# Chunk-selected attention and a softplus MLP: from two phases to one interleaved stream, with head pairs, 256-query steps, casting loads and one activation table

## The chip, the cores and the metric

The kernel runs on one core of one Trainium2 chip. The metric is device time in microseconds (us) of that core, given as the median of the runs of a kernel. Engines are named as in the profile: PE is TensorE, PEld its weight loads, DVE is VectorE, ACT is ScalarE, POOL is GpSimd, SP is SyncE. Lines such as L282 are lines of the kernel's source file; in experiments that add lines the numbers shift by a few.

## The reference, cut to what matters

There are 4 batches of 8 heads, 768 positions and 64 columns per head. Each query may attend to 6 chunks of 32 keys, picked by an upper bound on its scores; the result goes through a 512 to 2048 to 512 MLP with a softplus.

```python
ub = sum(maximum(q * k_min, q * k_max), axis=-1)      # per query and chunk of 32 keys
ub = where(causal_chunk, ub, -1e9)
top_chunks = argsort(ub)[..., -6:]
scores = scale * q @ k.T
scores = where(selected & causal, scores, -1e9)
attn = softmax(scores)
x = (attn @ v) laid out as 3072 tokens x 512
h = x @ w_in                                          # 512 x 2048
g = maximum(h, 0) + log1p(exp(-abs(h)))               # softplus
out = g @ w_out                                       # 2048 x 512
```

## The kernel before: the parts that matter

Attention runs head by head, and after it the MLP runs in blocks of 512 tokens. Both weights are loaded first, as float32, in front of the first q, k and v.

```python
# weights first, float32, then cast on DVE  (... cut)
nc.sync.dma_start(out=w_in_f32, in_=...); nc.vector.tensor_copy(w_in_sb, w_in_f32)
nc.sync.dma_start(out=w_out_f32, in_=...); nc.vector.tensor_copy(w_out_sb, w_out_f32)

# attention, for each of 32 heads, after its setup (... cut), 6 tiles of 128 queries
for tj in range(g0, g1):
    nc.tensor.matmul(at_ps[...], Kaug[0:KK, ...], Qaug[0:KK, ...], start=True, stop=True)
nc.vector.tensor_add(at_ps[diagonal], at_ps[diagonal], ltri)
nc.scalar.activation(attnT[...], at_ps[...], ACT.Exp)
for tj in range(g0, g1):
    nc.tensor.matmul(o_ps, attnT[...], v_aug[:, tj, :], start=(tj == 0), stop=(tj == t))
nc.vector.reciprocal(rrec, o_ps[:, D:D + 1])
nc.scalar.activation(o_sb, o_ps[:, 0:D], ACT.Copy, bias=0.0, scale=rrec)
nc.tensor.transpose(oT_ps, o_sb, ident)

# MLP, after all attention: 6 blocks of 512 tokens
for fg in range(KFF // 2):
    # 8 matmuls of 512 columns into hp (... cut)
    nc.scalar.activation(e_sb, hp, ACT.Exp)
    nc.scalar.activation(gT[...], e_sb, ACT.Ln, bias=1.0)
# then 4 x 16 matmuls with w_out, a copy and a store (... cut)
```

Exp and ln alternate on ACT in the MLP, and the compiled program loads an activation table before nearly each of them.

Of the kernel before, what the change touches and what calls it, by code (L numbers as in the profile page):

```python
# [17 lines left out]
def kernel(  # L18
# [14 lines left out]
    NQT = S // 128  # L33
    scale = 1.0 / math.sqrt(D)
    NEG = -30000.0
# [3 lines left out]
    assert d_model == H * D  # L39
    KDM = d_model // 128  # L40
    KFF = d_ff // 128

    ROWS = D + 1 + NCH

    singles = ctx.enter_context(tc.tile_pool(name="singles", bufs=1))
    ident = singles.tile([128, 128], BF16)
    make_identity(nc, ident)

    ltri = singles.tile([128, 128], F32, name="ltri")
    nc.gpsimd.memset(ltri, 0.0)  # L50
    nc.gpsimd.affine_select(out=ltri, in_=ltri, compare_op=ALU.is_ge, fill=NEG,
                            base=0, channel_multiplier=-1, pattern=[[1, 128]])

    ohb = singles.tile([32, S], BF16, name="ohb")
    nc.gpsimd.memset(ohb, 1.0)
# [3 lines left out]
                            base=CH - 1, channel_multiplier=CH, pattern=[[-1, S]])  # L59

    NKA = 3
    Kaugs = []
    for i in range(NKA):
        ka = singles.tile([128, S], BF16, name=f"Kaug{i}")
        nc.gpsimd.memset(ka[D:D + 64, :], 1.0)
        nc.sync.dma_start(out=ka[D + 1:D + 1 + NCH, :], in_=ohb[0:NCH, :])
        Kaugs.append(ka)

    xT = []
    for p in range(KDM):  # L70
        t = singles.tile([128, NTOK], BF16, name=f"xT_{p}")
        xT.append(t)

    w_in_f32 = singles.tile([128, KDM, d_ff], F32, name="w_in_f32")
    nc.sync.dma_start(out=w_in_f32,
                      in_=moe_w_in.rearrange("(kt ki) f -> ki kt f", ki=128))
    w_in_sb = singles.tile([128, KDM, d_ff], BF16, name="w_in_sb")
    nc.vector.tensor_copy(w_in_sb, w_in_f32)

    w_out_f32 = singles.tile([128, KFF, d_model], F32, name="w_out_f32")  # L80
    nc.sync.dma_start(out=w_out_f32,
                      in_=moe_w_out.rearrange("(kt ki) f -> ki kt f", ki=128))
    w_out_sb = singles.tile([128, KFF, d_model], BF16, name="w_out_sb")
    nc.vector.tensor_copy(w_out_sb, w_out_f32)

    attn_ctx = ExitStack()
    bh_pool = attn_ctx.enter_context(tc.tile_pool(name="bh", bufs=3))
    tp_psum = attn_ctx.enter_context(tc.tile_pool(name="tp_psum", bufs=2, space=bass.MemoryType.PSUM))
    at_psum = attn_ctx.enter_context(tc.tile_pool(name="at_psum", bufs=2, space=bass.MemoryType.PSUM))
    sm_psum = attn_ctx.enter_context(tc.tile_pool(name="sm_psum", bufs=2, space=bass.MemoryType.PSUM))  # L90
    work = attn_ctx.enter_context(tc.tile_pool(name="work", bufs=6))
    work2 = attn_ctx.enter_context(tc.tile_pool(name="work2", bufs=8))

    def do_setup(b, h, bh_idx):
        Kaug = Kaugs[bh_idx % NKA]
        q_f = bh_pool.tile([128, NQT, D], F32, name="q_f")
        nc.sync.dma_start(out=q_f, in_=q[b, h].rearrange("(t s) d -> s t d", s=128))
        k_f = bh_pool.tile([128, NQT, D], F32, name="k_f")
        nc.sync.dma_start(out=k_f, in_=k[b, h].rearrange("(t s) d -> s t d", s=128))
        v_f = bh_pool.tile([128, NQT, D], F32, name="v_f")  # L100
        nc.sync.dma_start(out=v_f, in_=v[b, h].rearrange("(t s) d -> s t d", s=128))

        k_b = bh_pool.tile([128, NQT, D], BF16, name="k_b")
        nc.vector.tensor_copy(k_b, k_f)
        v_aug = bh_pool.tile([128, NQT, D + 1], BF16, name="v_aug")
        nc.scalar.copy(v_aug[:, :, 0:D], v_f)
        nc.gpsimd.memset(v_aug[:, :, D:D + 1], 1.0)

        Qraw = bh_pool.tile([128, NQT, ROWS], BF16, name="Qraw")
        nc.scalar.copy(Qraw[:, :, 0:D], q_f)  # L110

        qT_ps = tp_psum.tile([D, S], BF16, name="qT_ps", tag="tp")
        kT_ps = tp_psum.tile([D, S], BF16, name="kT_ps", tag="tp")
        q_b_ap = Qraw[:, :, 0:D]
        for t in range(NQT):
            nc.tensor.transpose(qT_ps[:, t * 128:(t + 1) * 128],  # L116
                                q_b_ap[:, t, :], ident)
            nc.tensor.transpose(kT_ps[:, t * 128:(t + 1) * 128],  # L118
                                k_b[:, t, :], ident)
        qT = bh_pool.tile([D, S], BF16, name="qT")  # L120
        nc.vector.tensor_copy(qT, qT_ps)
        nc.scalar.activation(Kaug[0:D, :], kT_ps, ACT.Copy, bias=0.0, scale=scale)

        kmaxT = bh_pool.tile([D, NCH], BF16, name="kmaxT")
        kminT = bh_pool.tile([D, NCH], BF16, name="kminT")
        kT3 = Kaug[0:D, :].rearrange("d (c g) -> d c g", g=CH)
        nc.vector.tensor_reduce(kmaxT, kT3, axis=AX.X, op=ALU.max)  # L127
        nc.vector.tensor_reduce(kminT, kT3, axis=AX.X, op=ALU.min)  # L128

        qposT = bh_pool.tile([D, S], BF16, name="qposT")  # L130
        qnegT = bh_pool.tile([D, S], BF16, name="qnegT")
        nc.vector.tensor_scalar_max(qposT, qT, 0.0)
        nc.vector.tensor_scalar_min(qnegT, qT, 0.0)

        ub_ps = sm_psum.tile([128, NQT, NCH], F32, name="ub_ps", tag="sm")
        for t in range(NQT):
            qs = slice(t * 128, (t + 1) * 128)
            nc.tensor.matmul(ub_ps[:, t, :], qposT[:, qs], kmaxT,
                             start=True, stop=False)
            nc.tensor.matmul(ub_ps[:, t, :], qnegT[:, qs], kminT,  # L140
                             start=False, stop=True)
        ub_sb = bh_pool.tile([128, NQT, NCH], F32, name="ub_sb")
        nc.vector.tensor_copy(ub_sb, ub_ps)
        nc.gpsimd.affine_select(
            out=ub_sb, in_=ub_sb, compare_op=ALU.is_ge, fill=NEG,
            base=0, channel_multiplier=1, pattern=[[128, NQT], [-CH, NCH]])

        m8 = bh_pool.tile([128, NQT, 8], F32, name="m8")
        for t in range(NQT):
            nc.vector.max(out=m8[:, t, :], in_=ub_sb[:, t, :])  # L150
        nc.vector.tensor_scalar_mul(Qraw[:, :, D:D + 1], m8[:, :, 0:1], -1.0)
        ltm = bh_pool.tile([128, NQT, NCH], F32, name="ltm")
        nc.vector.tensor_tensor(
            ltm, ub_sb, m8[:, :, TOPK - 1:TOPK].to_broadcast([128, NQT, NCH]),
            op=ALU.is_lt)
        nc.vector.tensor_scalar_mul(Qraw[:, :, D + 1:D + 1 + NCH], ltm, NEG)

        Qaug_ps = tp_psum.tile([ROWS, S], BF16, name="Qaug_ps", tag="tp")
        for t in range(NQT):
            nc.tensor.transpose(Qaug_ps[:, t * 128:(t + 1) * 128],  # L160
                                Qraw[:, t, :], ident)
        Qaug = bh_pool.tile([128, S], BF16, name="Qaug")
        nc.scalar.copy(Qaug[:ROWS, :], Qaug_ps)

        return dict(Kaug=Kaug, Qaug=Qaug, v_aug=v_aug, h=h, b=b)

    def do_qtiles(st):
        Kaug, Qaug, v_aug, h, b = st["Kaug"], st["Qaug"], st["v_aug"], st["h"], st["b"]
        for t in range(NQT):
            nchk = (t + 1) * 4  # L170
            kcols = (t + 1) * 128
            KK = D + 1 + nchk

            attnT = work.tile([128, NQT * 128], BF16, name="attnT", tag="attnT")
            o_ps = sm_psum.tile([128, D + 1], F32, name="o_ps", tag="sm")
            for g0 in range(0, t + 1, 4):
                g1 = min(g0 + 4, t + 1)
                at_ps = at_psum.tile([128, 512], F32, name="at_ps", tag="at")
                for tj in range(g0, g1):
                    nc.tensor.matmul(  # L180
                        at_ps[:, (tj - g0) * 128:(tj - g0 + 1) * 128],
                        Kaug[0:KK, tj * 128:(tj + 1) * 128],
                        Qaug[0:KK, t * 128:(t + 1) * 128], start=True, stop=True)
                if g0 <= t < g1:
                    nc.vector.tensor_add(  # L185
                        at_ps[:, (t - g0) * 128:(t - g0 + 1) * 128],
                        at_ps[:, (t - g0) * 128:(t - g0 + 1) * 128], ltri)
# [19 lines left out]
    for i, (b, h) in enumerate(bhs):  # L207
        cur = do_setup(b, h, i)
        if prev is not None:
            do_qtiles(prev)  # L210
        prev = cur
    do_qtiles(prev)

    attn_ctx.close()

# [63 lines left out]
```

## Time and profile before

| | before |
|---|---|
| median of 3 runs | 688.14 us (687.73 to 689.16) |
| attention, by the timeline | about 27 to 392 us |
| MLP | about 392 to 687 us |
| ACT busy | 432.2 us, of which 106.5 us are table loads |
| PE busy | 494.0 us |

The first lines of the page give the busy time of each engine, and the busy share in 40 equal slices of the span (tenths, 9 is 90% or more). PEclk is the clock granted to PE, in tenths.

```profile
span 687.0 us, 9091 instructions
PE 494.0 (72%) x3248; PEld 276.2 (40%) x3264; DVE 275.9 (40%) x1114; ACT 432.2 (63%) x756; POOL 20.3 (3%) x78
...
PE   0178887778777887888787874965956956757647
...
ACT  0256666567566666666665599199297495693890
...
PEclk9999999755555555555555577897987988988978
```

No engine is full in the first half: from 40 to 380 us PE is busy for 82% and ACT for 62%. In the second half PE and ACT take turns. The chain of work that ended last says the same: it passes among three engines.

```profile
PE 43%; ACT 30%; DVE 18%; issue 6%; POOL 1%; ACTq 0%; DVEq 0%; POOLq 0%
```

The costliest groups give line, engine, operation, output and input, count, then busy us and mean ns, then the idle time of the engine before them and its releaser.

```profile
L197 ACT ACTIVATE o_sb<-o_ps,rrec 128x64 bf16<-128x64 f32 x192 | 59.6, 312 | 80.1 <-DVE rrec L195 79.9
L237 ACT ACTIVATE e_sb<-hp 128x1024 f32<-128x1024 f32 x48 | 48.5, 1022 | 72.1 <-PE hp L231 71.6
...
L231 PE MATMUL hp<-xT_81,w_in_sb 128*128 128x512 bf16 x96 | 40.7, 424 | 47.8 <-ACT e_sb L237 47.2
...
L238 ACT ACT_TABLE_LOAD x42 | 53.9, 1283 | 0.8
L237 ACT ACT_TABLE_LOAD x41 | 52.6, 1283 | 0.7
```

There are 83 table loads of 1.283 us within the MLP. ACT hardly idles before them (0.8 and 0.7 us in all), so they are work, not waiting. The timeline of one step of the MLP's first half-block shows what this does (start, duration, engine, line, operation; in brackets the idle time before it and who ended it).

```profile
404.42 1.28 ACT L237 ACT_TABLE_LOAD   x1
405.71 1.02 ACT L237 ACTIVATE e_sb<-hp 128x1024 f32<-128x1024 f32 x1
406.75 1.28 ACT L238 ACT_TABLE_LOAD   x1
406.79 0.38 PE L231 MATMUL hp<-xT_81,w_in_sb 128*128 128x512 bf16 x1 [2.82 <-ACT e_sb L237]
...
408.05 1.06 ACT L238 ACTIVATE gT<-e_sb 128x1024 bf16<-128x1024 f32 x1
...
408.48 0.63 PE L231 MATMUL hp<-xT_83,w_in_sb 128*128 128x512 bf16 x1
408.91 0.63 PE L231 MATMUL hp<-xT_84,w_in_sb 128*128 128x512 bf16 x1
```

ACT takes 4.6 us for two blocks of 128 hidden columns, more than half of it table loads. PE waits 2.8 us for it. Then the first matmuls follow at 0.215 us for 512 columns, and from 408 us on at 0.43. The Trainium skill ("TensorE: Matmul & The Clock Gate", section "Wait — 56ns, not 53.3ns?") gives start-to-start times of 426.7 ns for 512 columns while the array is cold and 215.7 ns once it is warm, and 106.7 and 55.6 ns for 128. This agrees: 0.43 us here, and the attention's score matmuls ran at about 0.107 us per 128 columns, cold (four of them took 0.62 us at 62.3 us, a single one about 0.30, so (0.62 - 0.30) / 3). The PEclk row still shows 0.9 at 62.3 us. The same page (section "Seeing it yourself") warns that its clock events have been seen to be unreliable.

### The profile page before, as it was taken

The page shows a single profiled execution, that of the slowest core. Times are in us where ns is not written, and L with a number is a line of the kernel's source. Part 1 is how long each engine was busy: PE and PEld are TensorE (multiplying, and loading weights), DVE is VectorE, ACT ScalarE, POOL GpSimd, SP SyncE. Part 2 cuts the span into 40 slices and gives each one's busy share as a digit, 9 for nine tenths or more (in the row PEclk, how much of TensorE's full clock was granted, in tenths as well). Part 3 has the DMA queues.
Part 4 walks back from the last instruction along what each step waited for, and adds up shares of the span by engine and source line. Part 5 has one row for each costly group of instructions (what it writes and reads, how often), then busy time and mean ns, then how long its engine had stood idle before and what let it go on. Part 6 is the DMA issues. An engine that isn't in the chain of part 4 may idle for free.

```text
span 687.0 us, 9091 instructions
## 1 busy us (share of the span) xinstructions
PE 494.0 (72%) x3248; PEld 276.2 (40%) x3264; DVE 275.9 (40%) x1114; ACT 432.2 (63%) x756; POOL 20.3 (3%) x78
## 2 busy tenths in 40 slices
PE   0178887778777887888787874965956956757647
PEld 0155555555555555555555421421422422313213
DVE  1576767676767676676767400100100100001001
ACT  0256666567566666666665599199297495693890
POOL 3000000000000000000000000000000000000000
PEclk9999999755555555555555577897987988988978
DMA  9963222222223221321000000100100100001001
GB/s 336 290 109 72 59 49 56 49 62 54 47 48 70 47 54 40 70 55 39 13 1 1 0 1 0 61 1 0 62 0 15 47 0 31 31 0 46 16 0 61
DMA packets 81465, 34.25 MB, mean 50 GB/s; under 512 B 75716, under 2 KB 75788, under 8 KB 80908
## 3 DMA queue, kind: packets, MB, share of 16 engines
q1 hardware_dynamic: 81420, 33.67, 18.9%
q8 instruction: 25, 0.41, 0.3%
q14 instruction: 20, 0.16, 0.1%
HBM read 27.26 MB, written 6.29 MB: 49 GB/s over the span
## 4 chain that ended last, share of the span: by engine, by line
PE 43%; ACT 30%; DVE 18%; issue 6%; POOL 1%; ACTq 0%; DVEq 0%; POOLq 0%
PE op L242 12%; ACT L238 8%; PE at_ps L180 7%; ACT e_sb L237 7%; ACT L237 7%; ACT gT L238 6%; PE o_ps L191 6%; PE oT_ps L199 5%; PE qT_ps L116 4%; DVE kminT L128 4%; PE Qaug_ps L160 4%; DVE kmaxT L127 4%; DVE at_ps L185 2%; PE kT_ps L118 2%; PE hp L231 2%
## 5 line engine op out<-in xcount | busy, mean ns | idle before, releaser
L242 PE MATMUL op<-w_out_sb,gT 128*128 128x512 bf16 x376 | 100.5, 425 | 40.7 <-ACT gT L238 40.3
L246 DVE COPY mo_sb<-op 128x512 f32<-128x512 f32 x24 | 16.6, 692 | 275.1 <-PE op L242 268.3
L188 ACT ACTIVATE attnT<-at_ps 128x512 bf16<-128x512 f32 (+3 forms) x256 | 109.2, 447 | 24.4 <-PE at_ps L180 17.1
L197 ACT ACTIVATE o_sb<-o_ps,rrec 128x64 bf16<-128x64 f32 x192 | 59.6, 312 | 80.1 <-DVE rrec L195 79.9
L237 ACT ACTIVATE e_sb<-hp 128x1024 f32<-128x1024 f32 x48 | 48.5, 1022 | 72.1 <-PE hp L231 71.6
L191 PE MATMUL o_ps<-v_aug,attnT 128*128 128x65 bf16 x672 | 85.4, 241 | 5.2 <-ACT attnT L188 4.5
L199 PE MATMUL oT_ps<-ident,o_sb 128*64 128x128 bf16 x192 | 59.8, 313 | 40.1 <-ACT o_sb L197 39.6
L231 PEld LDWEIGHTS <-w_in_sb 128*128 128x128 bf16 x384 | 41.1, 107 | 108.0 <-issue 73.6
L242 PEld LDWEIGHTS <-gT 128*128 128x128 bf16 x384 | 39.5, 107 | 102.4 <-ACT gT L238 50.9
L231 PE MATMUL hp<-xT_81,w_in_sb 128*128 128x512 bf16 x96 | 40.7, 424 | 47.8 <-ACT e_sb L237 47.2
L191 PEld LDWEIGHTS <-attnT 128*128 128x128 bf16 x672 | 47.0, 118 | 44.9 <-ACT attnT L188 17.5
L116 PE MATMUL qT_ps<-ident,Qraw 128*64 128x128 bf16 x192 | 38.8, 313 | 26.6 <-ACT Qraw L110 26.6
L185 DVE TENSOR_TENSOR at_ps<-at_ps,ltri 128x128 f32<-128x128 f32 x192 | 53.7, 288 | 6.8 <-PE at_ps L180 1.7
L238 ACT ACT_TABLE_LOAD x42 | 53.9, 1283 | 0.8
L237 ACT ACT_TABLE_LOAD x41 | 52.6, 1283 | 0.7
L199 PEld LDWEIGHTS <-o_sb 128*64 128x64 bf16 x192 | 25.7, 134 | 67.9 <-ACT o_sb L197 58.2
L238 ACT ACTIVATE gT<-e_sb 128x1024 bf16<-128x1024 f32 x48 | 50.0, 1054 | 0.5
L231 PE MATMUL hp<-xT_83,w_in_sb 128*128 128x512 bf16 x96 | 41.8, 436 | 0.7 <-issue 0.7
L195 DVE RECIPROCAL rrec<-o_ps 128x1 f32<-128x1 f32 x192 | 30.9, 161 | 24.7 <-PE o_ps L191 21.3
L180 PE MATMUL at_ps<-Qaug,Kaug_75 89*128 89x128 bf16 (+5 forms) x231 | 40.5, 305 | 0.2 <-ACT attnT L188 0.2
L180 PE MATMUL at_ps<-Qaug,Kaug_72 89*128 89x128 bf16 (+5 forms) x231 | 39.1, 304 | 0.6 <-ACT attnT L188 0.6
L231 PE MATMUL hp<-xT_84,w_in_sb 128*128 128x512 bf16 x92 | 39.6, 430 | 0.0
(151 smaller groups left out, 649.2 us busy)
## 6 DMA issues: line engine op xcount, KB each, us to landing
q_f<-in_q_dram SPq DMA_DIRECT2D x32, 192.0 KB, 2.8
k_f<-in_k_dram SPq DMA_DIRECT2D x32, 192.0 KB, 2.7
v_f<-in_v_dram SPq DMA_DIRECT2D x32, 192.0 KB, 2.8
out_dram<-mo_sb SPq DMA_DIRECT2D x24, 256.0 KB, 2.0
w_in_f_85<-in_moe_w_in_dram SPq DMA_DIRECT2D x1, 4096.0 KB, 12.9
w_out_f_89<-in_moe_w_out_dram SPq DMA_DIRECT2D x1, 4096.0 KB, 16.9
Kaug_72<-ohb SPq DMA_DIRECT2D x1, 36.0 KB
Kaug_75<-ohb SPq DMA_DIRECT2D x1, 36.0 KB
```

Source lines behind the costliest of these rows:

```text
L116: nc.tensor.transpose(qT_ps[:, t * 128:(t + 1) * 128], q_b_ap[:, t, :], ident)
L180: nc.tensor.matmul(at_ps[:, (tj - g0) * 128:(tj - g0 + 1) * 128], Kaug[0:KK, tj * 128:(tj + 1) * 128], Qaug[0:KK, t * 128:(t + 1) * 128], ...
L185: nc.vector.tensor_add(at_ps[:, (t - g0) * 128:(t - g0 + 1) * 128], at_ps[:, (t - g0) * 128:(t - g0 + 1) * 128], ltri)
L188: nc.scalar.activation(attnT[:, g0 * 128:g1 * 128], at_ps[:, :(g1 - g0) * 128], ACT.Exp)
L191: nc.tensor.matmul(o_ps, attnT[:, tj * 128:(tj + 1) * 128], v_aug[:, tj, :], start=(tj == 0), stop=(tj == t))
L195: nc.vector.reciprocal(rrec, o_ps[:, D:D + 1])
L197: nc.scalar.activation(o_sb, o_ps[:, 0:D], ACT.Copy, bias=0.0, scale=rrec)
L199: nc.tensor.transpose(oT_ps, o_sb, ident)
L231: nc.tensor.matmul(hp[:, fi, :], w_in_sb[:, dt, ft * 128:(ft + 1) * 128], xT[dt][:, cs], start=(dt == 0), stop=(dt == KDM - 1))
L237: nc.scalar.activation(e_sb, hp, ACT.Exp)
L238: nc.scalar.activation(gT[:, fg * 2:fg * 2 + 2, :], e_sb, ACT.Ln, bias=1.0)
L242: nc.tensor.matmul(op, gT[:, ft, stt * 128:(stt + 1) * 128], w_out_sb[:, ft, :], start=(ft == 0), stop=(ft == KFF - 1))
```

## The change

Its intent is to make one stream in which MLP matmuls fill the gaps of attention, and to take work off ACT and DVE:

- One activation table that holds exp, ln and copy is loaded once.
- q, k and v of two heads form a pair. They are loaded by casting DMAs on POOL's queue, straight to bf16; the weights too, w_in after the third pair and w_out in the second pair's preparation.
- The chunk bounds of both heads are one matmul against block-diagonal chunk maxima and minima. The chunk mask is a part of the score matmul: one-hot rows stand in the key tile, and masks in the query tile.
- Scores come in steps of 256 queries; the causal diagonal is zeroed by POOL after the exp; the normalising division moved to DVE.
- MLP blocks are 256 tokens, and the program emits MLP pieces between attention pieces by a cost ratio.

```diff
+    nc.scalar.preload_act_table_set("natural_log_exp_and_others")
+    def load(i):                          # load_v(i) likewise
+        for h in range(2):
+            nc.gpsimd.dma_start(out=k_sb[:, :, h, :], in_=k[b, 2 * p + h].rearrange(...))
+            nc.gpsimd.dma_start(out=q_sb[:, :, h, :], in_=q[b, 2 * p + h].rearrange(...))
...
+    for i in range(NV):                   # NV = 12 tiles of V with a column of ones
+        nc.vector.memset(v_sb[i][:, :, :, D:D + 1], 1.0)
+    for i in range(NK):                   # NK = 8 key tiles per head of a pair
+        nc.vector.tensor_copy(KA[i][64:96, :], ohb)
+        nc.vector.memset(KB[i][0:32, :], 0.0)
+        nc.vector.tensor_copy(KB[i][32:64, :], ohb)
+    load(1); load_v(1); load(2); load_v(2)      # after load(0), load_v(0)
+    for kt in range(KDM):
+        nc.gpsimd.dma_start(out=w_in_sb[:, kt, :], in_=moe_w_in[...])
...
+    def prep_pair(i):
+        # 6 transposes of k, max and min per chunk on DVE, key copies on ACT
+        for m, dst in enumerate((kmx, kmn)):
+            for h in range(2):
+                nc.gpsimd.tensor_copy(dst[h * 64:(h + 1) * 64, h], kx[h * 64:(h + 1) * 64, m])
+        yield 0.35
+        # 6 transposes of q; load(i + 3), load_v(i + 3); w_out if i == 1; qpos, qneg on DVE
+        # 12 matmuls: bounds ub; top-6 threshold and masks on DVE; 6 transposes of the masks
...
+    def score_step(st):
+        # two matmuls of up to 256 columns, one exp of 384 or 512 columns, repeated
+        nc.scalar.activation(pt[...], s_ps[:, 0:n], ACT.Exp, scale=scale)
+        nc.gpsimd.affine_select(out=diag, in_=diag, compare_op=ALU.is_ge, fill=0.0, ...)
...
+    RATIO = 1.75
+    def pump(cost):
+        state["attn"] += cost
+        while state["mlp"] < state["attn"] * RATIO - LAG:
+            c = next(mlp, "end")
...
```

An MLP block needs the outputs of all four pairs of its batch, so the MLP can't begin before the fourth pair is prepared.

## The prediction

> **What bounds the kernel now.** Two phases in series. In the windows view attention runs from 26.6 us (PE's first instruction, its loads queued behind 8 MB of weights) to about 383 us, the MLP from there to 687. From 40 to 380 us PE is busy 82%, DVE 70%, ACT 62%, at the cold pitch (128 columns per 0.107 us in the timeline). The chain of waits alternates PE, DVE, ACT inside each 128-query tile. In the MLP's first half-block ACT is the limit: table load 1.28, exp 1.02, load 1.28, ln 1.06 us per 1024 columns; 83 reloads are 106.5 us of ACT's 432. ACT also waits 72 us for the first matmuls of each block (waits view).
>
> **What the change does, costed from the trace.**
> - One table: removes 106.5 us of ACT, nearly all on the path.
> - ACT: the forms fit 0.165 us + 0.00084 per column. 96 exps of 384 (0.488) and 96 of 512 (0.596) are 104 us, 32 key copies (0.8) 26, 96 MLP exps of 512 57, 48 ln 51: 238 us, from 432. The 192 output scalings (59.6), casts (33) and Qaug copies (25) leave ACT.
> - PE: MLP is 384 matmuls at the warm 512-column pitch 0.215 plus 768 at half that (estimate): 166 us. Attention, at warm pitch, my estimate: 85 us, with half the transposes. 250 us, if warm.
> - DVE: about 6.8 us per pair of preparation, 0.9 per step, 0.7 per output: about 175 us, from 276.
> - GpSimd: 96 masks and 64 small copies, about 50 us, plus issuing 104 casting loads, which no trace here shows. The Trainium skill ("DMA: Bandwidth & Descriptors", SWDGE vs HWDGE vs iDMA) says a casting DMA must come from GpSimd, whose cores compute the descriptors. 1 to 2 us each is my guess, so 150 to 250 us of GpSimd.
> - Overlap: MLP matmuls fill attention's gaps; the sum of two latency-bound phases becomes the longest engine plus ramp.
>
> **The sum.** Loads, the preparations of four pairs (DVE 27 us, serial through PE, DVE and GpSimd) and 4 MB of w_in ahead of the fourth pair let the MLP start at about 55 to 65 us, with some 20 us of PE work done. The remaining 230 us run at about 85% of PE, since ACT (218 us left) is nearly as loaded and PSUM has only two score and two h buffers and one each for o and y: 270 us. Tail (last h chunks and outputs, PE-bound, partly in that): about 15. Predicted 345 us, range 300 to 405. Faster by over 2%: 0.97; within 2%: 0.01; slower: 0.02.
>
> **What shows each step.** One table load; ACT busy 230 to 250, PE 250 to 300 by the page, DVE 160 to 190. The 512-column pitch 0.215 in mid-run and a granted clock above 0.9 after 70 us. The chain mostly PE and ACT. First MLP matmul at 50 to 70 us.
>
> **What would make it wrong.** (1) Descriptor generation: at 3 us or more per load GpSimd has 350 us or more and becomes the limit, masks queued behind loads; it would lead the chain of waits. (2) A cold PE: the skill ("TensorE: Matmul & The Clock Gate", Part 1) puts the half-rate clock down to idle windows; this trace agrees, as first MLP matmuls go from 0.215 to 0.43 pitch after a 2.8 us gap. If the interleaved stream pauses often, PE needs up to 500 us. (3) In-order PE waiting on single buffers: 380 or more. (4) A better-packed stream: 300.

## More of the kernel before

The timeline has the last transpose of attention at 391.7 us and the first MLP matmul at 392.3 us.

## The result, and the profile after

| | before | after |
|---|---|---|
| median of the same rounds | 687.93 us (4 runs) | 351.00 us (350.19 to 352.25, 4 runs) |
| ratio | | 0.5104, 95% interval 0.509 to 0.5117 |
| PE busy | 494.0 | 281.8 |
| DVE busy | 275.9 | 171.5 |
| ACT busy | 432.2 | 218.1 |
| POOL busy | 20.3 | 140.1 |

A ratio is the mean time of one kernel's fast runs over that of the other's fast runs of the same rounds, so it isn't quite the ratio of the medians.

The same lines of the page, after. Rows for POOL and for DMA (the busy share of the DMA engines) are added, since both have become part of the story.

```profile
span 350.5 us, 7076 instructions
PE 281.8 (80%) x2784; PEld 202.2 (58%) x2784; DVE 171.5 (49%) x580; ACT 218.1 (62%) x369; POOL 140.1 (40%) x274
...
PE   1003254389889989999999899999999999999994
...
ACT  1102022259879749677987596879876878876640
POOL 8994877961682744350514443101112211000000
PEclk9999999999999999999999999999999999999999
DMA  9999999990795864443703444000000000000111
```

From the ninth slice on PE is busy for 80% or more. Before that, for some 70 us, PE is under 60% and POOL is the busiest of the engines in the sum. The DMA engines are at 90% or more for the first 79 us. The windows view puts numbers to it (window, its length, then busy us and instruction count of PE, PEld, DVE, ACT and POOL, the granted clock, the DMA share and GB/s).

```profile
0.00:80.00 80.00, 28.43 (x231) 20.63 (x232) 46.03 (x156) 17.77 (x29) 63.62 (x105) 1.00 1.40 122
...
100.00:320.00 220.00, 209.66 (x2171) 152.04 (x2171) 107.96 (x367) 171.28 (x296) 67.55 (x152) 1.00 0.32 40
```

PE is busy for 209.66 of 220 us in mid-run, and for 28.43 of the first 80. The chain of work that ended last names all engines.

```profile
PE 49%; POOL 16%; ACT 15%; DMA 7%; issue 7%; DVE 4%; POOLq 0%; ACTq 0%; DVEq 0%
```

In order of time (start, us, what), all of the chain's DMA lies in the first 77 us. It is two pieces, each from the issue of a weight to its landing:

```profile
21.89 11.92 DMA w_in_sb<-in_moe_w_in_dram
41.75 13.20 DMA w_out_sb<-in_moe_w_out_dram
```

They are 25 of these 77 us, and POOL's work is 33; the other 25 us of POOL's share are spread over the stream. After the first piece POOL issues its next load, having paused for 2.0 us. So the transfers of the weights, or full DMA engines, are a rival to POOL's order as the cause of the late start. No run takes the weights out; what the other runs say of it stands after the table of starts.

PE's waits of the first 80 us (engine, what it was for, releaser: us in all, times, longest) name the work on POOL.

```profile
PE ub L182 <- POOL bd_0_151 L151: 14.2, 1, 14.2
PE ub L182 <- POOL bd_1_153 L151: 7.6, 1, 7.6
PE o_ps L244 <- POOL pt L229: 7.3, 5, 3.4
```

The first is the block-diagonal copy of the first pair, a copy of 0.2 us. POOL's timeline shows why it came at 22.4 us: it stood behind the issue of the loads of the second and third pair and of w_in. (Not POOL alone held PE up: the other operand, qpos, was ready only at 21.52 us, since on DVE it stood behind the copies of the one-hot rows.)

```profile
18.27 1.88 POOL L86 DMA_DIRECT2D v_100<-in_v_dram  x2
20.14 2.29 POOL L127 DMA_DIRECT2D w_in_sb<-in_moe_w_in_dram  x4
22.41 0.47 POOL L151 COPY bd_0_151<-kx 64x24 bf16<-64x24 bf16 x2
```

The MLP's first matmul came at 55.42 us, but it was one alone. The unbroken stream begins at 77.07 us, and there the pitch changes from cold to warm.

```profile
78.35 0.42 PE L282 MATMUL hp<-xT_222,w_in_sb 128*128 128x256 bf16 x1
78.56 0.42 PE L282 MATMUL hp<-xT_223,w_in_sb 128*128 128x256 bf16 x1
...
79.62 0.27 PE L282 MATMUL hp<-xT_223,w_in_sb 128*128 128x256 bf16 x1
79.73 0.27 PE L282 MATMUL hp<-xT_224,w_in_sb 128*128 128x256 bf16 x1
```

256 columns take 0.21 us from start to start at 78.4 us, and 0.11 us at 79.6 us. The granted clock reads 1.00 for the whole start, so here too the pitch tells what the column doesn't.

The groups that answer those of before:

```profile
L225 ACT ACTIVATE pt<-s_ps 128x512 bf16<-128x512 f32 (+1 forms) x192 | 99.6, 544 | 69.3 <-PE s_ps L223 68.2
L297 PE MATMUL y<-w_out_sb,g 128*128 128x512 bf16 x384 | 100.4, 379 | 1.6 <-DVE y_sb L302 1.6
...
L284 ACT ACTIVATE e_sb<-hp 128x512 f32<-128x512 f32 x96 | 57.0, 597 | 37.3 <-PE hp L282 36.5
...
L286 ACT ACTIVATE g<-e_sb 128x1024 bf16<-128x1024 f32 x48 | 50.8, 1059 | 0.5
...
L77 POOL DMA_DIRECT2D k_sb<-in_k_dram x32 | 27.3, 855 | 25.5 <-PE kT L142 21.3
```

The waits have become one-sided. Before, ACT's exps of the MLP waited for PE (71.6 us) and PE waited for ACT's exps (47.2 us). Now the exps still wait for PE (36.5 us), while PE idles for 0.4 us in all before the matmuls of that layer. Issuing one load costs POOL 0.855 us.

### The profile page after: what moved, and what is told of

It is laid out like the page before. It is cut to its first block, busy times and chain, and to the rows that moved or that the text cites. A ratio compares the mean times of both kernels' runs of the same rounds, so it can differ in the third digit from the quotient of the medians.

```text
span 350.5 us, 7076 instructions
## 1 busy us (share of the span) xinstructions
PE 281.8 (80%) x2784; PEld 202.2 (58%) x2784; DVE 171.5 (49%) x580; ACT 218.1 (62%) x369; POOL 140.1 (40%) x274
## 3 DMA queue, kind: packets, MB, share of 16 engines
q0 software_dynamic: 77952, 13.64, 49.7%
## 4 chain that ended last, share of the span: by engine, by line
PE 49%; POOL 16%; ACT 15%; DMA 7%; issue 7%; DVE 4%; POOLq 0%; ACTq 0%; DVEq 0%
PE hp L282 18%; PE y L297 15%; ACT pt L225 6%; PE o_ps L244 5%; ACT e_sb L284 4%; DMA w_out_sb<-in_moe_w_out_dram 4%; POOL k_sb L77 4%; PE s_ps L220 4%; POOL q_sb L79 4%; ACT g L286 3%; DMA w_in_sb<-in_moe_w_in_dram 3%; POOL pt L229 3%; PE s_ps L223 2%; PE mT L202 2%; PE kT L142 1%
## 5 line engine op out<-in xcount | busy, mean ns | idle before, releaser
L225 ACT ACTIVATE pt<-s_ps 128x512 bf16<-128x512 f32 (+1 forms) x192 | 99.6, 544 | 69.3 <-PE s_ps L223 68.2
L297 PE MATMUL y<-w_out_sb,g 128*128 128x512 bf16 x384 | 100.4, 379 | 1.6 <-DVE y_sb L302 1.6
L229 POOL TENSOR_SCALAR_AFFINE_SELECT pt<-pt 128x256 bf16<-128x256 bf16 x96 | 38.8, 409 | 127.2 <-ACT pt L225 126.1
L284 ACT ACTIVATE e_sb<-hp 128x512 f32<-128x512 f32 x96 | 57.0, 597 | 37.3 <-PE hp L282 36.5
L282 PEld LDWEIGHTS <-w_in_sb 128*128 128x128 bf16 x768 | 72.4, 99 | 13.4 <-issue 1.2
L282 PE MATMUL hp<-xT_221,w_in_sb 128*128 128x256 bf16 x192 | 53.1, 277 | 0.0
L282 PE MATMUL hp<-xT_222,w_in_sb 128*128 128x256 bf16 x192 | 52.7, 276 | 0.0
L282 PE MATMUL hp<-xT_223,w_in_sb 128*128 128x256 bf16 x192 | 52.3, 275 | 0.0
L282 PE MATMUL hp<-xT_224,w_in_sb 128*128 128x256 bf16 x192 | 51.6, 275 | 0.4
L286 ACT ACTIVATE g<-e_sb 128x1024 bf16<-128x1024 f32 x48 | 50.8, 1059 | 0.5
L244 PEld LDWEIGHTS <-pt 128*128 128x128 bf16 x672 | 33.5, 99 | 27.9 <-POOL pt L229 20.0
L297 PEld LDWEIGHTS <-g 128*128 128x128 bf16 x384 | 34.5, 97 | 25.6 <-issue 2.1
L77 POOL DMA_DIRECT2D k_sb<-in_k_dram x32 | 27.3, 855 | 25.5 <-PE kT L142 21.3
L182 PE MATMUL ub<-bd_0_151,qpos 128*128 128x48 bf16 x48 | 4.4, 191 | 15.4 <-POOL bd_0_151 L151 14.2
```

The lines of the kernel that those rows point to most:

```text
L77: nc.gpsimd.dma_start(out=k_sb[:, :, h, :], in_=k[b, 2 * p + h].rearrange("(t s) d -> s t d", s=128))
L225: nc.scalar.activation(pt[:, h, j:j + 2].rearrange("k j c -> k (j c)")[:, 0:n], s_ps[:, 0:n], ACT.Exp, scale=scale)
L229: nc.gpsimd.affine_select(out=diag, in_=diag, compare_op=ALU.is_ge, fill=0.0, base=0, channel_multiplier=-1, pattern=[[0, 2], [1, 128]])
L244: nc.tensor.matmul(o_ps[:, u, h], pt[:, h, j, c0:c0 + 128], v_sb[i % NV][:, j, h, :], start=(j == 0), stop=(j == t0 + u))
L282: nc.tensor.matmul(hp[:, fi], w_in_sb[:, dt, ft * 128:(ft + 1) * 128], xT[dt][:, cs], start=(dt == 0), stop=(dt == KDM - 1))
L284: nc.scalar.activation(e_sb[:, f2 * 2:f2 * 2 + 2], hp, ACT.Exp)
```

## The experiments

Twelve kernels ran, and all of them gave correct results. Times are medians of 4 runs beside the kernel before on the same chip (687.2 to 688.5 us in these rounds).

| run | time us | ratio to before | 95% |
|---|---|---|---|
| after | 351.0 | 0.5104 | 0.509 to 0.5117 |
| e1_before_one_table | 572.2 | 0.8321 | 0.8294 to 0.8349 |
| e2_after_two_tables | 464.8 | 0.6746 | 0.6706 to 0.6786 |
| e3_after_serial | 358.5 | 0.5206 | 0.5183 to 0.5229 |
| e8_forced_serial | 413.3 | 0.5993 | 0.5961 to 0.6025 |
| e4_bd_on_dve | 343.4 | 0.4994 | 0.4978 to 0.5011 |
| e5_qkv_on_sp | 343.9 | 0.4995 | 0.4983 to 0.5007 |
| e9_start | 342.1 | 0.4972 | 0.4963 to 0.498 |
| e10_start_sp | 346.1 | 0.5033 | 0.5023 to 0.5043 |
| e11_start_late | 340.1 | 0.4948 | 0.4937 to 0.4958 |
| e12_sp_wide5 | 344.0 | 0.5016 | 0.4992 to 0.504 |
| e13_memset_first | 340.4 | 0.4944 | 0.4933 to 0.4956 |
| e14_masks_on_dve | 330.2 | 0.4797 | 0.4786 to 0.4809 |

Two questions were asked: what each part of the change is worth (e1, e2, e3, e8), and what holds up the start (the others).

### The table alone, put into the kernel before

```diff
+    nc.scalar.preload_act_table_set("natural_log_exp_and_others")
```

> The kernel before with nothing changed but one activation table for the whole run. Theory (the 83 table loads of 1.283 us stand in series on ACT, and ACT paces the MLP's first half-block): the MLP loses about 105 us, 688 becomes 575 to 600 us; attention stays at 26.6 to about 383 us. Rival (the loads are mostly hidden behind matmuls): less than 60 us is gained, 630 us or more.

It took 572.2 us, 115.9 us less than the kernel before in the same rounds (688.1) and a little below the range expected. The two windows below are attention and MLP of this kernel.

```profile
40.00:380.00 340.00, 276.30 (x2379) 185.53 (x2378) 237.29 (x1038) 212.59 (x545) 14.22 (x60) 0.61 0.21 47
400.00:570.00 170.00, 161.84 (x741) 71.24 (x738) 16.59 (x24) 90.05 (x93) 0.00 (x0) 1.00 0.10 38
```

Attention is as before (PE 276.30 us in 40 to 380, against 277.3 before). The MLP now is limited by PE, which is busy for 161.84 of 170 us, at clock 1.00. The saving is 9 us larger than the 106.5 us of the 83 loads. PE's pauses went with the loads, and its clock in the MLP rose from 0.83 to 0.86 before to 1.00. The pitch says the same: 126 pairs of MLP matmuls in succession were at the cold pitch before and 7 in this run, of some 750. That the clock made the 9 us fits, but no run separates it.

### The table alone, taken out of the kernel after

```diff
-    nc.scalar.preload_act_table_set("natural_log_exp_and_others")
```

> The kernel after without its preloaded common table: 96 table loads instead of 1. Theory (an interleaved stream needs the one table): ACT gets 122 us more, about 340 us busy, becomes the longest engine, and the time is 400 to 440 us. Rival (ACT was idle 38% of the time, so the loads fit into that idle time): 375 us or less.

It took 464.8 us, 113.8 us more than after and above the range that was expected. The trace has 96 table loads, 95 more than after: 121.9 us of ACT. ACT was busy for 290.44 of the 340 us from 100 to 440 us, and PE waited for it.

```profile
PE s_ps L218 <- ACT pt L223: 67.8, 38, 4.2
```

So the loads cost the interleaved stream nearly as much time as they take: ACT with both tables' loads is fuller than PE (342.8 us busy against 316.8). A part of PE's time is itself a consequence: PE was busy for 281.8 us in the kernel after, and here 124 pairs of MLP matmuls were at the cold pitch instead of 11. The rival reading, that interleaving would hide the loads, falls.

### Emitting the MLP after attention

```diff
-    RATIO = 1.75
+    RATIO = 0.0
```

> The kernel after with the MLP emitted after all attention (the ratio set to 0), so the same instructions, not interleaved. Theory (overlap is a main part of the gain): attention alone is bound by waits at a low matmul clock and takes 200 to 240 us, the MLP alone about 170 us at the full clock, 390 to 420 us in all. Rival (the leaner instructions and the table make the gain, overlap little): 370 us or less.

It took 358.5 us, only 7.5 us more. This did not answer the question it was made for: the trace shows the MLP's first matmul at 56.4 us all the same, although the program emits all of the MLP after attention. The framework's scheduler decides the order on PE, and moved the MLP up. What the run does show is that the hand-set pacing is worth some 2%, over that scheduler's own order. The next run forces the order by data instead.

### A truly serial version

Every block of w_in is rewritten (plus zero times the last attention output), so that no MLP matmul can start before attention ends.

```diff
-    RATIO = 1.75
+    RATIO = 0.0
+    nc.vector.tensor_scalar_mul(zero, xT[NP - 1][:, NTOK - 1:NTOK], 0.0)
+    w4 = w_in_sb.rearrange("p k (f c) -> p k f c", c=128)[:, :, :, 0:1]
+    nc.vector.tensor_tensor(w4, w4, zero(broadcast), op=ALU.add)     # after the last output
```

> The kernel after with the MLP truly behind attention: the earlier try left the order to the scheduler, which interleaved anyway, so here every weight block of the first layer is rewritten (plus zero) after the last attention output, and no MLP matmul can start before. Theory (overlap is worth a lot): attention alone ends at 205 to 235 us, the MLP then takes about 170 us at the full clock, 375 to 410 us in all, and the granted clock or the matmul pitch is at half rate in attention. Rival (overlap is worth little, the leaner instructions make the gain): 362 us or less.

It took 413.3 us, a little above the range expected, so the overlap is worth 62 us. Its windows, two of attention and one of the MLP, show what overlap buys.

```profile
76.00:150.00 74.00, 57.44 (x645) 41.86 (x643) 53.23 (x207) 47.71 (x90) 46.28 (x93) 0.79 0.71 47
150.00:228.00 78.00, 61.10 (x735) 44.33 (x734) 51.31 (x190) 54.10 (x105) 29.65 (x75) 0.82 0.16 11
240.00:411.00 171.00, 165.87 (x1125) 109.59 (x1123) 16.61 (x24) 105.55 (x142) 0.00 (x0) 1.00 0.10 38
```

Alone, attention keeps PE at about 78% with a granted clock near 0.8. The pitch of its transposes from 76 to 228 us agrees that PE was cold in a part of the time: 65 pairs in succession were cold and 117 warm. PE was busy for 316.9 us in this run and for 281.8 us in the kernel after, on the same matmuls. So of the 62 us, some 35 us are matmuls that run faster when the MLP keeps PE busy, and the rest are gaps that are filled (the split is worked out from the two busy times, and a busy time contains overlapping matmuls, so it is rough).

Taken together, in this order: one table 688 to 572 us, all other edits 572 to 413, overlap 413 to 351. The terms depend on the order; removing the table from the other end cost 114 us, nearly the same. The middle term, 159 us, is the largest, and it is a remainder that no run takes apart. The traces only say where it lies: against e1_before_one_table, attention in e8_forced_serial starts 19 us sooner (7.2 us instead of 26.4) and is 139 us shorter (227 us instead of 366), while the MLP is 2 us shorter. In attention PE was busy for 146 us instead of 291, DVE for 151 instead of 253 and ACT for 120 instead of 226. How much of this belongs to the pairs, the mask in the matmul, the longer steps, the casting loads or the moved division stays open.

### The block-diagonal copies on VectorE

```diff
-                nc.gpsimd.tensor_copy(dst[h * 64:(h + 1) * 64, h], ...)
+                nc.vector.tensor_copy(dst[h * 64:(h + 1) * 64, h], ...)
```

> The kernel after with the four small block-diagonal copies of a pair on VectorE instead of GpSimd. Theory (in the first 76 us PE waits for these copies, which stand behind load instructions in GpSimd's order): the first ub matmul moves from 22.9 to about 13 us, the dense MLP begins 10 to 18 us earlier, the time is 333 to 342 us. Rival (the start waits for the bytes of the loads, or for VectorE's chain): within 1% of 351 us.

It took 343.4 us, 7.6 us less. The 14.2 us wait did not go away; it got another owner.

```profile
25.65 0.22 PE L182 MATMUL ub<-bd,qpos 128*128 128x48 bf16 x1 [17.00 <-DVE qpos L171]
```

On VectorE the one-hot copies stand before the first pair's query copies, and 8 of the 16 took about 0.8 us, where in the kernel after they had taken 0.35 or 0.56. So the first bound matmul came later than in the kernel after (25.65 us instead of 22.93). The gain came from the later pairs, which followed 8.7 to 10.9 us apart (9.8 to 14.7 us in the kernel after).

### q, k and v as float32 over SP's queue

```diff
+    def load_cast(dst, src, i):                    # staging pool of 2
+        for h in range(2):
+            nc.sync.dma_start(out=f[:, :, h, :], in_=src[b, 2 * p + h]...)
+        nc.gpsimd.tensor_copy(dst, f)
```

> The kernel after with q, k and v loaded as f32 by the SP queue and cast on GpSimd by one 128x768 copy per tile, in place of 96 casting loads; the weights stay casting loads. Theory (the casting path, 0.85 us of GpSimd each and 36 ns of a DMA engine per packet, makes the start long): the DMA share of the first 80 us falls clearly, the dense MLP starts 10 to 20 us sooner, 330 to 342 us. Rival (the start is set by VectorE's serial chain, and casts cost GpSimd as much as issues): 346 us or more.

It took 343.9 us, 7.1 us less. So against this alternative the casting loads are a small loss. The DMA share of the first 80 us fell from 1.40 to 0.81 as the theory asked, but the unbroken MLP stream began only 2.9 us sooner, not 10 to 20; the rest of the gain came later. A packet cost the DMA engines more on POOL's queue: 49.7% of 16 engines over 350.5 us for 77952 packets is 35.8 ns of an engine's time each, against 30.1% of 343.0 us for 78720 packets, or 21.0 ns, on SP's queue here (weights are in the first mean and outputs in the second). Whether the casting or the queue makes the difference isn't separated.

### The start, with the copies on ScalarE

The block-diagonal copies go to ACT, and the one-hot rows are put in place by SP's DMAs.

```diff
-        nc.vector.tensor_copy(KA[i][64:96, :], ohb)       # KB likewise
+        nc.sync.dma_start(out=KA[i][64:96, :], in_=ohb)
-                nc.gpsimd.tensor_copy(dst[...], kx[...])
+                nc.scalar.copy(dst[...], kx[...])
```

> The kernel after with the block-diagonal copies on ACT, which is idle at the start, and the 16 copies of the one-hot rows moved from VectorE to loads on the SP queue. Theory (the start is bound by what stands in order on VectorE and GpSimd): the first ub matmul comes at 14 to 16 us instead of 22.9, the dense MLP at 55 to 62 us instead of 76, 328 to 338 us. Rival (the loads' arrival bounds the start): 343 us or more.

It took 342.1 us, between the two theories. The first bound matmul came at 13.86 us instead of 22.93, and the next two 8.9 and 9.3 us later, but the fourth only after another 15.0 us. There PE waited for the causal masks, which POOL does between load issues:

```profile
43.34 0.81 PE L244 MATMUL o_ps<-v,pt 128*128 128x65 bf16 x6 [4.17 <-POOL pt L229]
```

### Both at once

e9_start's edit and e5_qkv_on_sp's edit together.

> The edits of both previous runs together. If the two limits are in series, the gains add up to 315 to 328 us; if one hides the other, the time is that of the better one within 3 us.

It took 346.1 us: the two gains don't add. SP's queue now holds the 16 one-hot DMAs in front of the loads:

```profile
27.00 0.40 PE L223 MATMUL s_ps<-qa,ka 96*128 96x256 bf16 x1 [8.24 <-DMA ka<-ohb]
38.41 0.82 PE L159 MATMUL qT<-ident,q_sb 128*128 128x128 bf16 x6 [8.93 <-POOL q_sb L80]
```

### One-hot rows lazily, w_in later

```diff
-        nc.vector.tensor_copy(KA[i][64:96, :], ohb)       # KB likewise, all at the start
+        if i < NK: nc.scalar.copy(ka[64:96, :], ohb)      # in prep_pair; kb likewise
-    for kt in range(KDM): nc.gpsimd.dma_start(w_in ...)   # before the fourth pair's loads
+        if i == 0: for kt in range(KDM): nc.gpsimd.dma_start(w_in ...)   # in prep_pair, after them
```

The block-diagonal copies are on ACT as in e9_start.

> The block-diagonal copies go to ScalarE, the one-hot rows are copied by ScalarE just before each pair needs them, and the w_in loads are issued after the fourth pair's q, k, v loads instead of ahead of everything. Theory (what holds up the start is the order of work on GpSimd: copies and weight loads ahead of the later pairs' loads and masks): the dense MLP matmuls start at 55 to 62 us instead of 76, time 328 to 337 us. Rival (GpSimd's load issues and the masks behind them still set the pace, or ScalarE now delays exps): dense MLP not before 68 us, time 340 us or more.

It took 340.1 us, and the unbroken MLP stream began at 65.5 us: better than e9_start (67.3 us), but neither the time nor the start that the theory asked for. The rival's time came true (340 or more), and its start (68 or later) did not. PE's waits for the masks on POOL between 40 and 90 us still summed to 6.2 us.

### The same with SP's queue and five staging tiles

> Block-diagonal copies on ScalarE, one-hot rows on GpSimd just before each pair, w_in late, and q, k, v loaded as float32 by the SP queue into five staging tiles with the cast on GpSimd (the pool of V tiles is cut to 8 to make room). Theory (with the load issues gone from GpSimd and with cheaper packets the start is shorter than in e11_start_late): 322 to 335 us, below e11_start_late. Rival (after the copies are moved the start is limited by the VectorE chain of some 9 us per pair, or by staging tiles coming free, so the loads' queue doesn't matter): equal to e11_start_late within 1 percent, or slower, at 340 us or more.

It took 344.0 us, so the theory falls: SP's queue did not help here. The reading isn't clean. The pool of V tiles was smaller, and the one-hot copies were on POOL in this kernel, and one of them held PE up for 8.1 us, behind casts. The run shows that this arrangement is no better, not that no arrangement of SP loads can be.

### An earlier first step

```diff
+    for i in range(NV): nc.vector.memset(v_sb[i][:, :, :, D:D + 1], 1.0)   # moved up, before load(0)
```

> e11_start_late with the memsets of the ones columns of V ahead of the first V load. In e11_start_late VectorE's first reductions stood behind five memsets and one memset that waited for the first V load (9.3 us). Theory (a late step at the start delays everything after it): the first block-bound matmul at 12 us or earlier instead of 14, dense MLP at 59 to 60 us instead of 62, time 337 to 338.5 us. Rival (the fourth pair is paced by GpSimd's load issues and masks at 40 to 60 us, so an earlier start is lost there): within 1 us of e11_start_late, 339 to 341 us.

It took 340.4 us against 340.1 us of e11_start_late. The first bound matmul moved from 14.03 to 11.48 us as meant, and the gain was lost later, as the rival said: PE's waits for the masks on POOL in the first 90 us grew from 6.2 to 11.1 us. (The 62 us that the expectation gives for e11_start_late is an earlier mark than the 65.5 us used here, which is the start of six MLP matmuls in a row.)

### The first batch's masks on VectorE

```diff
-            nc.gpsimd.affine_select(out=diag, in_=diag, ...)
+            if i < NP: nc.vector.tensor_tensor(diag, diag, tri, op=ALU.mult)   # 0/1 triangle
+            else:      nc.gpsimd.affine_select(out=diag, in_=diag, ...)
```

> e13_memset_first plus the causal masks of the first four pairs on VectorE (a multiply by a 0/1 triangle) instead of on GpSimd behind the load issues. PE waited 6.2 us for these masks between 40 and 90 us in e11_start_late. Theory (those waits hold back the fourth pair): 331 to 336 us, dense MLP at 54 to 58 us. Rival (the waits only move to VectorE, which carries the prep of the next pair, or the pairs' loads are what is late): within 1 percent of e13_memset_first.

It took 330.2 us, 10.2 us less than e13_memset_first and 20.8 us less than the kernel after: a ratio of 0.4797 to before, the best. PE's waits for the masks in the first 90 us, first in e13_memset_first and then in e14_masks_on_dve:

```profile
PE o_ps L247 <- POOL pt L232: 11.1, 6, 3.2
```

```profile
PE o_ps L254 <- DVE pt L237: 4.1, 5, 1.3
```

A mask costs VectorE 0.283 us and POOL some 0.41 us, but the point is the queue before it: on POOL it stood behind load issues of 0.85 us each.

### What the start experiments say together

For each of these runs the table gives the start of the first unbroken stretch of six or more MLP matmuls of the first layer, read from PE's timeline, and the span of the profiled run less that start.

| run | unbroken MLP from, us | span, us | rest, us |
|---|---|---|---|
| after | 77.1 | 350.5 | 273.4 |
| e5_qkv_on_sp | 74.2 | 343.0 | 268.8 |
| e10_start_sp | 71.4 | 343.3 | 271.9 |
| e12_sp_wide5 | 70.4 | 342.3 | 271.9 |
| e4_bd_on_dve | 68.6 | 342.0 | 273.4 |
| e9_start | 67.3 | 340.3 | 273.0 |
| e13_memset_first | 65.7 | 338.8 | 273.1 |
| e11_start_late | 65.5 | 338.7 | 273.2 |
| e14_masks_on_dve | 56.8 | 329.7 | 272.9 |

The start varies by 20 us. Where the loads stay on POOL's queue, the rest is 272.9 to 273.4 us, so all that these edits gained or failed to gain was in the time before the unbroken stream. In the three runs with loads on SP's queue the rest is shorter too, by 1.5 us or, in e5_qkv_on_sp, by 4.6 us, which is more than its start gained (2.9 us). Why is not tested.

The DMA engines being full does not explain the start by itself: e5_qkv_on_sp cut their share of the first 80 us to 0.81 for 2.9 us of start, and e14_masks_on_dve gained 20 us of start at a share of 1.50. What the landing of the weights costs stays open. In e14_masks_on_dve the chain still has 6.9 us of w_in and 9.4 us of a V load before 42 us.

## Why the prediction was right, point by point

**The total was right (345 predicted, 351.0 measured), through two errors of opposite sign, so partly by luck.** The sum was 60 us of start, 270 us of stream and 15 us of tail. The start was 77 us, and all that followed took 273 us, tail included. The start was mis-sized by 17 us, and the stream with its tail, which was counted again after it, by 12 us the other way (285 predicted, 273 measured). The range of 300 to 405 us was wider than the knowledge that stood behind it, once the trace had given the pitches.

**One table: right in kind, a little small.** The prediction said 106.5 us, nearly all on the path. Put into the kernel before it was worth 115.9 us, and taken out of the kernel after 113.8 us. The trace after has a single load.

**PE's work: right.** 250 us were estimated if warm, and 250 to 300 us were to be read from the page, which says 281.8. An estimate with the pitches of the new trace (384 matmuls at 0.2155 us, 768 at 0.109, the scores at 0.109 and 0.0556, the outputs at 0.029, transposes at about 0.055, bounds at 0.026) gives about 249 us. Some 11 us of that lie before the stream starts, and the other 238 us took 273 us, so the stream with its tail runs at 87% of these pitches. Predicted were 85% without the tail (230 of 270 us) and 81% with it (230 of 285 us). By the windows PE is 95% busy in mid-run. The page's busy time is larger than the pitch sum, since a matmul's record is longer than the pitch (0.379 us on average for 512 columns, against 0.2155) and the matmuls of the cold start count in full.

**ACT: the sum was right, the check was not.** 238 us were summed up, and the groups after sum to 234.0 us (99.6 + 57.0 + 50.8 + 25.3 of key copies + 1.3). The page was to show 230 to 250 us and shows 218.1 us, because successive instructions overlap on the engine and the page counts that time once. The same was true before (458.9 us by groups, 432.2 by the page), so "238 from 432" compared two kinds of figure.

**DVE: right** (160 to 190 us predicted, 171.5 measured).

**POOL: the guess was too high.** 1 to 2 us per load were guessed, with 150 to 250 us in all; it was 0.855 us per load, and 140.1 us in all. The skill ("DMA: Bandwidth & Descriptors", section "SWDGE vs HWDGE vs iDMA") says that POOL's cores compute the descriptors of these DMAs, and the trace agrees in that each issue holds POOL for that long. The first risk, 3 us a load, did not come. But the prediction tied masks queued behind loads to that cost and otherwise looked at POOL's sum, not at its order. In the start POOL is 80% busy (63.62 of 80 us), and small copies and masks of 0.2 to 0.4 us stand behind issues of 0.85 us. The runs e9, e11, e13 and e14 show what that order is worth: 20.8 us came back by moving those small operations, the one-hot rows, a memset and w_in, with the casting loads left where they were. The 57 us that are left of the start are not taken apart.

**The first MLP matmul: inside the range, and the wrong check.** It came at 55.42 us (50 to 70 predicted), but alone. The start of the unbroken stream was meant, and that was at 77 us. In e14_masks_on_dve the stream does start at 56.8 us. So the 55 to 65 us were within reach of this design but not of this order of instructions.

**A warm PE after 70 us: nearly right.** The pitch goes to 0.11 us per 256 columns at 79.6 us, right after the stream starts, and no later pair of MLP matmuls is at the cold pitch. The second risk, a cold PE, is what e8_forced_serial shows for a part of attention alone. But its reason, pauses, does not tell the two kernels apart: from 40 to 380 us of the kernel before 311 of 357 pairs of transposes in succession are at the cold pitch and none at the warm one, although PE never pauses for more than 1.1 us, and from 80 to 340 us of the kernel after 193 of 208 are warm and none is cold, with pauses as long (PE idle for 18% of the one stretch and 5% of the other). What decides it was not tested.

**The chain: right at its head** (PE 49%, ACT 15%), but POOL's 16% and DMA's 7% were not foreseen; over half of POOL's and all of DMA's are in the start.

**The third risk, single buffers, did not come**: PE's waits for one buffer of y were 1.6 us in the whole run.

What stays open: what the single edits within attention are worth, what the landing of the weights costs in the start, which part of the 13% between pitch sum and stream could be had, whether the 9 us that the table gave above its own time were the clock's doing, and whether loads on SP's queue would beat e14_masks_on_dve, if they didn't share the start with anything else.

## What to carry to other kernels

When phases are merged into one stream, sum up the fullest engine, and look at the start by itself: here the stream came out close to that sum and the larger error sat in the start. Write down the order of each in-order queue up to the first full step, above all on an engine that both issues loads and does small work that others wait for. Put the small work that gates a start onto an engine without long issues in its queue; here that was worth 21 us, while moving the loads themselves was worth 7 us alone, most of it after the start, and nothing clear on top. Test "how much is overlap worth" by a data dependence, not by the order in which the program emits things, since a scheduler may undo that order.

## What the Trainium skill lacked or had wrong

- "DMA: Bandwidth & Descriptors" (section "Anatomy of one DMA — SWDGE (gpsimd) path") gives a fixed 2.0 us plus bytes per DMA, and calls the making of descriptors small, but does not say how long an issue holds POOL; nearest is the 1 us to the first byte that the page puts down to it elsewhere. Here it was 0.855 us for a q or k load of one head, cast to bf16, and 0.58 to 0.76 us for a quarter of a weight.
- No page was found that says how long POOL can pause before an issue while earlier large loads are under way. The profile shows pauses of 1.5 to 2.0 us before loads, that end at a landing of w_in or w_out (for example 1.69 us before a V load at 31.5 us of the kernel after). The cause was not tested.
- "ScalarE: Activation LUTs" (section "What ACT_TABLE_LOAD costs") gives about 1283 ns for the load plus about 1380 ns of drain, 2.66 us per switch. The 1283 ns are in the trace to the digit, but the drain is not: ACT idled for 1.5 us in all before 83 loads, and 95 added loads cost 113.8 us, 1.2 us each.
- "TensorE: Matmul & The Clock Gate" (section "Part 4: PE-mode transpose") says that full clock doesn't engage for transposes. Within the warm stream of matmuls six transposes of 128 columns took 0.51 us at 201.2 us of the kernel after, about 0.058 us each after the first (taking 0.22 us for a single one), which is the warm pitch. Whether these transposes use the mode that the section speaks of can't be read from the trace, and no run has transposes alone.
- "SBUF — State Buffer" (section "SBUF: two separate sides") describes VectorE and POOL as excluding each other for whole instructions. The runs fit that, but the page's one timing of this is of a single POOL DMA beside a copy, not of many short instructions on both, and there the same work went two ways. In e2, e3, e4 and e8 VectorE's copies of 32 x 768, after the first one or two, took 0.80 to 0.82 us while POOL issued q, k and v loads, one copy for each issue of 0.81 us, and 0.35 to 0.44 us while it issued w_in. In the kernel after they took 0.35 and 0.56 us under the same loads, two for each issue of 0.94 us. What picks the one or the other was not tested.
